# Batch 1's time-shift mix moved from TensorE to VectorE in a fused attention and channel-mix kernel

## The chip, the cores and the metric

The kernel runs on one core of a Trainium2 chip. The metric is the device time of one execution in microseconds; the kernel before was timed three times, and the median stands for it. Engine names as in the profile: PE (TensorE matmul), PEld (its weight loads), DVE (VectorE), ACT (ScalarE), POOL (GpSimd), SP (SyncE, which here only issues DMAs).

## The reference

Eight batches, 8 heads, 576 positions, head size 64; d_model 512, d_ff 1024. Linear attention, and then a channel mix with a time shift:

```python
q_s = softmax(q over the head dimension); k_s = softmax(k over the positions)
kv  = einsum('bhsd,bhse->bhde', k_s, v)
x   = einsum('bhsd,bhde->bhse', q_s, kv)        # -> (B, S, 512)
x_prev = x shifted by one position, zeros first
xk = mu_k * x + (1.0 - mu_k) * x_prev
xr = mu_r * x + (1.0 - mu_r) * x_prev
k  = np.maximum(xk @ w_k, 0.0)
v  = k * k @ w_v
r  = 1.0 / (1.0 + np.exp(-(xr @ w_r)))
out = r * v
```

## The kernel before

**Groups and units.** Attention is worked off in 16 groups of four heads, named by batch and half: group 31 is batch 3, second half. The channel mix is worked off in ten units of 512 positions (two of 256) over rings of four batches, `xk` and `xr`. Unit 1 needs batches 0 and 1, unit 2 batches 1 and 2, and so on.

**Steps of a group** (b, g stand for batch and half, and a last 0 or 1 for a part):

- `load..q`, `load..k`, `load..v`: loads into the 11 buffers `raw`, two halves of 288 KB each for batches 0 and 1, one load of 576 KB for the others (issued by POOL from batch 1 on, L204).
- `expq`, `expk` (ACT, L328), `cast` of v (ACT, L334); `rsum`, `rrec`, `scale` (DVE): the softmax of q.
- `T`: 18 or 36 small transposes of q on PE (L367); `KV`: the products of k and v, which also give the sum of exp k (L397). In batch 0 they are separate; later both stand in one block, named `TKV` or `B`, in one PSUM buffer `att` (there are two).
- `rz`, `w` (DVE): kv divided by the sums; `qt` (ACT, L375): the transposed q out of PSUM. From batch 5 on q is transposed by a DMA that SP issues (L517), and `qt` is that DMA.
- `X` (PE, L537): x = w times qt, 8 matmuls. It rides in the block `B` of the next group, ahead of that group's transposes; for groups in `ALONE` it stands by itself (X21, X71).
- `xs`, `xb` (ACT, L546, L543): x out of PSUM; `edge`, `diff` (DVE, L551, L555): the shifted difference; four scalings by mu, `sc` (DVE, L560), and two adds, `mix` (DVE, L565), give `xk` and `xr`.

**Fused batches.** In batches 0 and 1 (`FUSED`) the mix is folded into the weights instead: DVE or POOL multiplies kv by mu and 1 - mu (`kvn`, `wp`, L475), PE computes xk and xr directly with 16 matmuls each (`X100`, `X101`, ..., L487), the shifted half reading qt one column earlier, and ACT and DVE copy the results out (`x1000`, `x1001`, ..., L497). Here `edge` is a copy within qt.

**Steps of a unit**: `k10` to `k17` (PE, L621, four matmuls of 128x512 each, in the first two units partly in two halves, the second named `k10.2`), `relu` (ACT, L608), `sq` (DVE, L612); `r10` to `r13` (PE, L653), `th` (ACT, L658); `v100`, `v101`, ... (PE, L673, four matmuls each; in unit 0 v is cut by `WV`), `o` (DVE, L679) and the stores `st` (SP, L689). The banks of PSUM for k, r and v are the four `mm`.

**Order.** Nothing is scheduled at run time: `ORDER` is a list of all steps written out. Each engine issues its own steps in the order of the list, and waits there for what a step needs. A number behind a step's name is the buffer that it takes. So a step that waits holds back everything behind it on its engine. `muload` fetches mu for the scalings, `mu` transposes it on PE, `mucopy` takes it out of PSUM.

The functions that the diff touches:

Of the kernel before, what the change touches and what calls it, by code (L numbers as in the profile page):

```python
# [8 lines left out]
ACT = mybir.ActivationFunctionType  # L9
# [21 lines left out]
WV = (0, 4, 6, 8)  # L31
# [5 lines left out]
FUSED = (0, 1)  # L37
EARLY_UNITS = 2
ALONE = ((2, 1), (B - 1, 1))
# [5 lines left out]
ACT!load00q0:0 zero ident load00q1 ACT!load00k0:1 load01q1:2 ACT!load01q0 rows load00v consts warm  # L45
load00k1 load01v late load01k0:3 load10q0:4 wk00 wk01 expq001:0 expq000 load11q0:5 rsum001:0
ACT!load01k1 rsum000 load10k0:6 expq011:1 rrec001 wk11 rrec000 rsum011:1 fill:1 fill.2:2 fill.3:3
fill.4:0 fill.5:1 fill.6:2 fill.7:3 fill.8:0 fill.9:1 fill.10:2 fill.11:3 fill.12:0 fill.13:1
fill.14:2 fill.15:3 fill.16:0 wide:0 scale000:0 expq010 expk000:0 rsum010 expk001 scale001
widecopy wk10 rrec010 fill.17:1 fill.18:2 KV001:0 rrec011 scale010:1 KV000 T00:1 rest Z00 qt00:0  # L50
scale011 rz00:0 expk010:1 fill.19:3 fill.20:1 fill.21:1 T01:3 edge00 kvn00:0 load10q1 expk011
fill.22:1 KV010:2 wp000:0 expq100:2 wr wp001 X000:1.0 qt01:1 KV011 x0001 Z01 load10k1 x0000 rz01:1
X001:0.3 kvn01:1 wp010:1 k02:0 x0010 edge01 k00:1 x0011 X010:1.0 load11q1 k03:2 x0100 x0101 k01:3
wv0 rsum100:2 k00.2 expk100:2 load10v1:7 k02.2 wp011 expq110:0 k03.2 relu00:0 k01.2 load10v0
X011:0.1 relu01:1 k07:1 sq01:0 load11v0:8 sq00 expq101 k05:3 load11v1 relu02:2 rsum101 relu03:1
k06:0 rrec100 sq02 relu05:0 sq03 x0110 k04:2 x0111 relu06:2 sq05 load11k1:9 r00:3 relu07:1
load11k0 expk101 r02:0 expq111 wv1 r03:1 relu04:0 rsum111:3 th00:0 r01:2 sq07 th03:1 sq04 rrec101
th02:2 scale101:2 v020:3 wv2 scale100 cast101:0 v030:1 load20v0:10 rrec111 cast100 scale111:0
muload v000:0 th01:3 rsum110 cast110:1 v010:2 load20q0:0 rrec110 cast111 scale110 TKV10:0
expk111:0 load21q0:2 expk110 load30q0:1 rz10:2 kvn10:0 TKV11:1 qt10:2 wp100:0 load20k0:3 v011  # L60
load21v0:4 rz11:0 sq06 v031 kvn11:1 edge10 qt11:0 v021 wp110:1 load61v0:6 v001 v032 edge11 v002
cast200:2 X100:0.1 load21k0:5 o00 v022 load31q0:7 x1001 x1000 v012 o02 expq200:1 wp111 mu:0
X110:1.0 mucopy k13:3 load30v0:8 x1101 x1100 k11:0 wp101 o01 expq210:2 k13.2 rsum200:0 k11.2
load31k0:9 relu13:1 X111:0.1 relu11:0 load40q0:10 k12:2 x1111 x1110 k17:3 o03 expk200:1 load30k0:0
sq11:1 k10:0 st03.2 sq13 k16:1 st00 expq300:0 rrec200 rsum210:1 load40v0:2 st03 X101:1.0 st01
relu17:2 k12.2 x1011 st00.2 x1010 k10.2 load31v0:3 sq17 relu16:0 k14:3 scale200:1 relu10:1
relu12:2 r12:1 cast210:0 sq10 load60q0:1 TKV20:0 rsum300:2 relu14:1 r11:0 th12:4 rrec210 rrec300
load41q0:4 rz20:1 expk210:2 k15:2 sq12 w20:0 scale210:2 r10:3 qt20:1 v120:1 sq16 relu15:2
scale300:0 expq310:1 B21:1.0 load50q0:5 sq14 th10:5 v110:2 rz21:2 sq15 xs20:0 xb20 w21:1
load40k0:7 rsum310:3 v100:3 qt21:0 v121 edge20 diff20:0 th11:6 v111 cast300:1 sc2000:0 X21:0.1  # L70
sc2011:1 o11 r13:0 xs21:1 load41k0:8 xb21 sc2010 o12 v101 expk300:0 edge21 rrec310 r20:2 diff21:1
expk310:1 load41v0:0 sc2001 v130:1 sc2101:2 mix200 th20:1 load60v0:9 TKV30:1 sc2100 th13:0
sc2111:0 mix210 v131 cast310:2 sc2110 k27:2 cast400:0 o13 load51q0:3 rz30:0 k21:0 scale310:1
st13.2 relu27:0 load50k0:2 st13 expq400:2 k22:1 o10 k20:2 w30:2 relu22:1 load71v0:10 st10 mix201
qt30:2 st11 k23:3 sq27:0 st11.2 rsum400:0 relu21:2 k24:1 st01.2 relu23:0 st10.2 B31:0.1 mix211
expk400:2 sq23 k26:0 rz31:1 relu24:0 rrec400 load50v0:7 sq21 xb30:0 w31:0 k25:3 sq24 scale400:2
relu20:2 r22:1 xs30 qt31:1 sq20 r23:2 edge30 diff30:0 relu25:0 B40:1.0 relu26:2 sq22 sc3001:2
expq410:0 v200:3 sc3000 mix300 th22:0 v220:0 load71k0:4 rz40:2 sq25 th23:6 rsum410:1 xs31:1 r21:1
xb31 v230:2 sq26 expq500:1 edge31 sc3011:1 v201 diff31:1 cast410:1 load61q0:5 w40:1 v231 sc3101:0
sc3100 th21:3 rrec410 load61k0:0 mix310 v221 expq510:2 o23 r30:1 o20 qt40:0 load71q0:3 k33:2  # L80
scale410:0 st20.2 th30:5 st20 k37:3 relu33:1 st12.2 o22 k40:1 st12 relu37:0 sc3111:2 v210:2 sc3010
st02 expk410:0 rsum500:2 st02.2 k41:0 k35:3 expq600:0 load51k0:8 mix301 v211 sc3110 relu40:2
load51v0:1 sq37:1 k32:1 relu35:0 o21 expk500:1 sq33 B41:0.1 mix311 relu41:1 load70q0:2 sq35 k31:3
rz41:0 sq40:0 relu32:0 w41:2 sq41 k30:2 sq32 relu31:2 rsum510:3 cast500:2 k34:0 r31:1 relu30:1
rsum600:0 load70v0:7 relu34:0 r33:3 th31:1 sq30 xs40:0 rrec510 k36:2 xb40 rrec500 sq31 sq34 k44:0
scale500:1 relu36:1 r32:1 relu44:2 k43:2 edge40 qt50:1 th32:4 diff40:0 v330:0 qt41:2 sq36 v310:1
rrec600 st23.2 sc4001:0 th33:2 scale510:2 v331 expq610:1 k46:3 sc4000 qt51:0 relu43:0 o33
load60k0:5 B50:1.0 relu46:1 cast510:0 scale600:0 k47:2 st23 k42:0 cast600:1 v300:3 load70k0:1 sq46
qt60:2 sq44 rz50:1 mix400 v311 relu47:1 xs41:1 xb41 v320:2 o31 relu42:2 sq47 v301 expq700:2 st31.2
edge41 sq42 diff41:1 st21 r41:1 st21.2 expk510:2 o30 v321 sc4101:1 st30.2 sc4100 sq43 st31 k45:0  # L90
sc4110:2 mix410 st30 r40:3 relu45:1 expk600:0 o32 v410:0 sq45 rsum610:1 th41:6 k50:2 sc4111 k52:1
relu50:2 w50:0 rsum700:2 cast610:2 v411 k51:2 relu52:0 o41 mix411 k53:1 relu51:1 rrec610 B51:0.1
sq51:1 sq50 k54:0 scale610:1 xb50:1 v400:2 relu53:1 sc4010:0 relu54:2 rz51:2 sq52 k55:1 expq710:0
sc4011 rrec700 mix401 v401 relu55:0 rsum710:3 k56:0 th40:3 expk610:1 k57:1 sq53 sq54 relu56:1 sq55
r50:3 w51:1 relu57:2 scale700:2 r51:0 th50:1 cast700:0 v500:1 rrec710 o40 sq56 v510:3 th51:5 st40
sq57 xs50 st41 edge50 B60:1.0 st33 diff50:1 v501 st32.2 xb51:0 sc5000:1 st41.2 rz60:0 sc5001 v511
xs51 st40.2 w60:2 expk700:2 mix500 qt61:1 r52:2 o50 expk710:0 o51 B61:0.1 st50 edge51 v520:0
st50.2 sc5010:2 diff51:0 th52:6 st22 r53:1 cast710:1 st51 sc5011 sc5100:0 st51.2 sc5101 v521
sc5110:1 th53:3 mix510 v530:3 sc5111 rz61:1 mix511 k60:2 o52 xb60:0 v531 w61:0 st52 mix501
relu60:0 st32 k61:1 scale710:0 xs60 st52.2 B70:1.0 st22.2 relu61:1 o53 k62:0 xb61:1 sq60:0 st53  # L100
edge60 k63:2 relu62:2 st53.2 diff60:1 xs61 st33.2 k64:1 sq61 relu63:0 qt70:0 sc6000:0 sc6001 k65:3
sc6010:1 relu64:1 mix600 k66:0 sq62 edge61 relu65:2 sq63 k67:2 diff61:0 relu66:0 r60:1 sq64
sc6100:2 relu67:1 sc6101 r61:3 sq65 th60:1 mix610 v600:0 sq66 th61:5 sc6011 sq67 v610:2 sc6110:0
sc6111 mix601 v601 mix611 v611 rz70:2 w70:1 r62:1 o60 o61 st60 r63:3 th62:4 st60.2 v620:0 st61
th63:6 v630:2 v621 v631 o62 k70:1 st62 o63 k71:3 relu70:2 st63 st63.2 k72:0 sq70:1 relu71:0 qt71:2
k73:2 sq71 relu72:1 k74:1 sq72 relu73:2 k75:3 sq73 relu74:0 k76:0 sq74 relu75:1 k77:2 sq75
relu76:2 r70:1 sq76 relu77:0 B71:0.1 sq77 th70:0 v700:3 xb70:0 rz71:0 w71:2 r71:0 v701 th71:3 xs70
v710:2 o70 edge70 X71:1.0 st70 diff70:1 v711 xb71:1 st70.2 sc7000:2 r72:1 sc7001 xs71 o71 r73:0
edge71 st71 th72:2 mix700 st71.2 v720:3 diff71:0 th73:1 sc7010:1 v730:2 sc7100:0 sc7101 sc7110:2
v721 mix710 sc7111 v731 sc7011 o72 k80:1 mix711 st72 k81:0 st72.2 o73 relu80:1 mix701 st73 k82:3  # L110
relu81:2 st73.2 sq80:0 k83:2 sq81 relu82:0 k84:1 sq82 relu83:1 k85:0 sq83 relu84:2 k86:3 sq84
relu85:0 k87:2 sq85 relu86:1 r80:1 sq86 relu87:2 r81:0 sq87 th80:5 v800:3 th81:4 v810:2 v801 v811
o80 r82:1 st80 o81 st80.2 r83:0 th82:6 st81 st81.2 v820:3 th83:0 v830:2 v821 v831 o82 k90:1 st82
o83 k91:0 st82.2 relu90:0 k92:3 st83 relu91:1 sq90:1 k93:2 relu92:2 sq91 st83.2 k94:1 relu93:0
sq92 k95:0 relu94:1 sq93 k96:3 relu95:2 sq94 k97:2 relu96:0 sq95 r90:1 relu97:1 sq96 sq97 r91:0
th90:3 v900:3 th91:2 v901 v910:2 o90 v911 st90.2 st90 v910.2:1 o91 v911.2 st91.2 st91 o91.2 st91.3
st91.4
"""


class Slot:

# [728 lines left out]
```

## Time and profile before

| | |
|---|---|
| three runs | 195.72, 196.65, 196.67 us; median 196.65 |
| profiled execution: span from first to last instruction | 194.9 us, 1.75 less than the median (its own time is not given besides the span) |
| granted PE clock | 1.00 throughout |
| PE, DVE, ACT, POOL busy | 184.8, 150.1, 141.0, 43.6 us |
| HBM | 33.56 MB read, 9.44 MB written |
| k of unit 0 begins (k02), X21, X71, last matmul | 15.6, 55.95, 158.6, 191.2 us |

The rows of the profile read: line, engine, operation, output<-inputs, shape, count, then busy time and mean, then the idle time of the engine before them and what ended it. A line of the timeline begins with start and duration. In the table by stage each engine has its busy microseconds and the number of instructions in brackets; then come the granted clock, the mean share of the 16 DMA engines, and GB/s. In the list of DMA issues the last number is the median time from issue to landing.

### The profile page before, as it was taken

The numbers are of one execution on the slowest core, as the hardware profiler recorded it, in microseconds if no ns is written. First come the engines' busy times: TensorE is split into PE (matmuls) and PEld (weight loads), VectorE is DVE, ScalarE is ACT, GpSimd is POOL, SyncE is SP. The second block draws the span as 40 slices with busy tenths as digits, with TensorE's granted clock in tenths as the row PEclk, the third lists the DMA queues.
The fourth block names the chain that finished last, engine by engine and source line by source line (L and its number), as shares of the span: only waits on it lengthen the run. The fifth ranks groups of instructions, "written<-read, shape, count | busy, mean of one in ns | idle before, by whom it ended". The sixth has DMA issues, their size and how long they took to land.

```text
span 194.9 us, 4739 instructions
## 1 busy us (share of the span) xinstructions
PE 184.8 (95%) x1849; PEld 90.6 (46%) x1873; DVE 150.1 (77%) x347; ACT 141.0 (72%) x218; POOL 43.6 (22%) x70
## 2 busy tenths in 40 slices
PE   7789999999999999999999999999999989999992
PEld 2264445435544554545554444444444434444751
DVE  1887668799999999989989998999924359622532
ACT  3788899899999999989996798677226632662340
POOL 8444457794324212241110000000000000000000
PEclk9999999999999999999999999999999999999999
DMA  6999999999999999999699604886039872403413
GB/s 185 322 263 294 268 346 302 402 393 394 411 389 392 392 408 335 290 366 316 143 217 124 203 0 108 170 190 146 0 73 116 56 89 54 111 0 79 95 43 108
DMA packets 23586, 41.86 MB, mean 215 GB/s; under 512 B 9344, under 2 KB 12684, under 8 KB 23564
## 3 DMA queue, kind: packets, MB, share of 16 engines
q0 software_dynamic: 9440, 27.99, 45.3%
q1 hardware_dynamic: 13308, 12.13, 28.4%
q10 hardware_dynamic: 816, 1.44, 2.0%
q8 instruction: 14, 0.23, 0.6%
q14 instruction: 8, 0.07, 0.1%
HBM read 33.56 MB, written 9.44 MB: 221 GB/s over the span
## 4 chain that ended last, share of the span: by engine, by line
PE 76%; DMA 15%; POOL 2%; issue 2%; ACT 1%; DVE 1%; POOLq 0%; DVEq 0%
PE mm_c L673 10%; PE mm_d L673 9%; PE mm_c L621 8%; PE mm_b L621 7%; PE mm_a L621 7%; PE mm_b L653 7%; PE mm_d L621 6%; DMA wk_ab<-in_moe_w_k_dram 6%; DMA wv_a<-in_moe_w_v_dram 5%; PE mm_a L673 5%; PE mm_b L673 4%; DMA raw_k<-in_v_dram 4%; PE mm_a L653 4%; PE mm_d L653 3%; PE mm_c L653 1%
## 5 line engine op out<-in xcount | busy, mean ns | idle before, releaser
L673 PEld LDWEIGHTS <-k_a 128*128 128x128 bf16 x144 | 13.8, 98 | 16.6 <-issue 0.5
L653 PEld LDWEIGHTS <-xr 128*128 128x128 bf16 x144 | 13.9, 98 | 16.1 <-issue 0.2
L673 PEld LDWEIGHTS <-k_b 128*128 128x128 bf16 x152 | 14.4, 98 | 15.0 <-issue 0.2
L653 PE MATMUL mm_b<-wr,xr 128*128 128x512 bf16 x62 | 16.3, 379 | 0.1
L621 PEld LDWEIGHTS <-wk_ab 128*128 128x128 bf16 x80 | 7.7, 98 | 8.3 <-issue 0.8
L621 PEld LDWEIGHTS <-wk_bb 128*128 128x128 bf16 x80 | 7.8, 98 | 7.7
L621 PEld LDWEIGHTS <-wk_aa 128*128 128x128 bf16 x80 | 7.4, 98 | 8.2 <-issue 0.9
L621 PEld LDWEIGHTS <-wk_ba 128*128 128x128 bf16 x80 | 7.5, 98 | 7.8 <-issue 0.2
L653 PE MATMUL mm_a<-wr,xr 128*128 128x512 bf16 x35 | 9.2, 380 | 0.1
L673 PE MATMUL mm_c<-wv_a,k_a 128*128 128x512 bf16 x32 | 8.2, 379 | 0.0
L608 ACT ACTIVATE rel_a<-mm_b 128x512 bf16<-128x512 f32 (+1 forms) x8 | 4.6, 579 | 4.2 <-PE mm_b L621 3.6
L608 ACT ACTIVATE rel_b<-mm_b 128x512 bf16<-128x512 f32 (+1 forms) x7 | 4.1, 585 | 4.9 <-PE mm_b L621 4.8
L621 PE MATMUL mm_c<-xk,wk_aa 128*128 128x512 bf16 (+1 forms) x26 | 7.3, 363 | 0.0
L612 DVE TENSOR_TENSOR k_a<-rel_b 128x512 bf16<-128x512 bf16 (+1 forms) x14 | 5.3, 382 | 2.5 <-ACT rel_b L608 2.5
L673 PE MATMUL mm_d<-wv_a,k_b 128*128 128x512 bf16 x26 | 7.1, 379 | 0.1
L653 PE MATMUL mm_d<-wr,xr 128*128 128x512 bf16 x28 | 7.2, 379 | 0.0
L621 PE MATMUL mm_c<-xk,wk_ab 128*128 128x512 bf16 (+1 forms) x24 | 6.9, 362 | 0.0
L612 DVE TENSOR_TENSOR k_b<-rel_a 128x512 bf16<-128x512 bf16 (+1 forms) x14 | 5.5, 392 | 1.8 <-ACT rel_a L608 1.3
L608 ACT ACTIVATE rel_c<-mm_a 128x512 bf16<-128x512 f32 (+1 forms) x11 | 6.2, 561 | 0.7 <-PE mm_a L621 0.7
L612 DVE TENSOR_TENSOR k_b<-rel_b 128x512 bf16<-128x512 bf16 (+1 forms) x14 | 5.5, 392 | 1.3 <-ACT rel_b L608 0.9
L612 DVE TENSOR_TENSOR k_b<-rel_c 128x512 bf16<-128x512 bf16 (+1 forms) x12 | 4.7, 392 | 1.9 <-ACT rel_c L608 1.6
L621 PE MATMUL mm_d<-xk,wk_bb 128*128 128x512 bf16 (+1 forms) x22 | 6.1, 360 | 0.1
(352 smaller groups left out, 532.3 us busy)
## 6 DMA issues: line engine op xcount, KB each, us to landing
out_dram<-th_b SPq DMA_DIRECT2D x12, 128.0 KB, 3.6
out_dram<-th_g SPq DMA_DIRECT2D x12, 128.0 KB, 5.2
out_dram<-th_d SPq DMA_DIRECT2D x11, 128.0 KB, 5.6
out_dram<-th_a SPq DMA_DIRECT2D x10, 128.0 KB, 2.7
raw_k<-in_v_dram POOLq DMA_DIRECT2D x2, 576.0 KB, 8.9
raw_c<-in_q_dram POOLq DMA_DIRECT2D x2, 576.0 KB, 7.0
raw_b<-in_q_dram POOLq DMA_DIRECT2D x2, 576.0 KB, 10.4
raw_f<-in_k_dram POOLq DMA_DIRECT2D x2, 576.0 KB, 7.9
```

The source lines that it names most:

```text
L608: kn.nc.scalar.activation(out=kn.rels[rel.index][:, 0:n], in_=kn.bank(kf)[:, 0:n], func=ACT.Relu, scale=HALF_ROOT)
L612: kn.nc.vector.tensor_tensor(out=kn.k2s[k2.index][:, fc, 0:n], in0=kn.rels[rel.index][:, 0:n], in1=kn.rels[rel.index][:, 0:n], op=ALU.mult)
L621: kn.nc.tensor.matmul(kn.bank(kf)[:, 0:n], lhsT=kn.wk[fc // 4][ct % 2][:, ct // 2, (fc % 4) * 128: (fc % 4) * 128 + 128], rhs=kn.xs[0][:, ...
L653: kn.nc.tensor.matmul(kn.bank(rps), lhsT=kn.xs[1][:, ct, c:c + 128], rhs=kn.wr[:, ct, :], start=(ct == 0), stop=(ct == CT - 1))
L673: kn.nc.tensor.matmul(kn.bank(vps)[:, 0:width], lhsT=kn.k2s[k2.index][:, ft, 128 * m:128 * m + 128], rhs=wv_of(ft)[:, part], start=(ft == ...
```

## The change

1. `FUSED` holds groups 00 and 01 only. Batch 1's groups take the steps of the later batches: `w`, `X` with 8 matmuls, `xs`, `xb`, `edge`, `diff`, four `sc`, two `mix`. X10 rides in the block B11; X11 stands alone.
2. The transposes of both groups of batch 1 go into one block (`SOON`): TKV10 holds the transposes of group 10, those of group 11 (into the other `att` buffer) and KV10. B11 holds X10 and KV11. The copy qt11 depends on TKV10 alone.
3. w_v is loaded in four pieces of two row blocks each, not three, and v of unit 0 is computed in four pieces per tile.
4. The loads of mu for the scalings go from POOL's queue to SP's, and they and `mu` stand earlier.
5. The whole `ORDER` is another one: loads, attention steps, unit steps and stores stand in other places, and other buffers are taken.
6. `HALF`, a mixed form, is empty and has no effect.

```diff
-WV = (0, 4, 6, 8)
+WV = (0, 2, 4, 6, 8)
-FUSED = (0, 1)
+FUSED = ((0, 0), (0, 1))
+HALF = ()
+SOON = {(1, 1): (1, 0)}
-ALONE = ((2, 1), (B - 1, 1))
+ALONE = ((1, 1), (2, 1), (B - 1, 1))
...
-            kn.nc.gpsimd.dma_start(out=kn.mu_sb[4 * m:4 * m + 4, :], in_=bass.AP(
+            kn.nc.sync.dma_start(out=kn.mu_sb[4 * m:4 * m + 4, :], in_=bass.AP(
...
-    mu_load = add("POOL", emit_mu_load, name="muload")
+    mu_load = add("SP", emit_mu_load, name="muload")
...
+        own = Slot("any" if b == 0 else "att")
+        turns[b, g] = [transpose_q, before_t, own, qs, None]
+        yield
+        soon = [turns[t] for t in SOON if SOON[t] == (b, g)]
+        done = turns[b, g][4]
...
-            qtp = kvp = Slot("att")
+            qtp = kvp = own
+            first_t = not crossed and not done
...
-                if not crossed:
+                if first_t:
                     transpose_q(qtp)
+                for t in soon:
+                    t[0](t[2])
                 kv(qtp)
...
-            qcopy = add("ACT", lambda: copy_qt(qtp), [tr, wdone], [qt], [qtp], name=f"qt{tag}")
+            qcopy = add("ACT", lambda: copy_qt(qtp), [done] if done else [tr, wdone], [qt], [qtp], name=f"qt{tag}")
```

The new order, around the steps that the prediction follows (batch 1's attention; then the loads of group 31 and X21):

```
... r00:2 r03:3 scale100 th00:0 scale111 cast100:0 sq05 mucopy th03:1 cast101 sq07 expk100 r01:0 r02:2
TKV10:1.0 v020:3 th01:2 expk110:0 sq06 cast111:1 cast110 rz10:2 w10:0 qt10:2 v000:1 load20k0:0 v030:0
load20q0:2 expk111 qt11:0 B11:1 rz11:0 v001 v021 w11:1 xs10:0 xb10 edge10 diff10:0 sc1001:0 load30q0:1
v031 sc1000 th02:3 load21k0:3 load41q0:4 load21q0:5 X11:0.1 xs11:1 v002 v003 o00 load21v0:7 xb11 v010:2
cast200:2 edge11 diff11:1 v011 v032 load30v0:6 v022 mix100 sc1101:1 load61q0:8 v033 v012 k12:1 expk200:1
v013 v023 expq200:1 load31q0:9 sc1100 o03 mix110 o02 o01 k13:0 k12.2 k13.2 ...
... th20:6 rsum300:3 sq14 expq310:1 B21:0.1 rz21:2 sq15 xb20:0 xs20 st03 r10:1 w21:0 v121 load40q0:9
qt21:2 rsum310:2 edge20 rrec300 v110:3 th12:2 X21:1.0 th10:3 v100:0 v101 ...
```

In the new order B71, r61, v600, v521, v620, v601, v621, r63, k75 and X71 follow each other on PE; in the old one B71, v700, r71, v701, v710 and X71. The eight stores of unit 0 (st03.2, st01.2, st01, st02, st00.2, st02.2, st00, st03) are the first stores on SP; in the old order five of them came first (st03.2, st00, st03, st01, st00.2), and the others behind stores of unit 1.

## The prediction

> **What bounds the kernel now.** I read the page first: its busy shares, then the 40 slices.
>
> ```profile
> span 194.9 us, 4739 instructions
> PE 184.8 (95%) x1849; PEld 90.6 (46%) x1873; DVE 150.1 (77%) x347; ACT 141.0 (72%) x218; POOL 43.6 (22%) x70
> ...
> PE   7789999999999999999999999999999989999992
> DVE  1887668799999999989989998999924359622532
> ...
> DMA  6999999999999999999699604886039872403413
> ```
>
> PE is full from about 15 us to 191 us, DVE from 40 to 140, the DMA engines from 5 to 90. So a PE microsecond saved counts only if DVE and the loads keep up. The table by stage gives DVE's reserve:
>
> ```profile
> 42.60:61.00 18.40, 18.08 (x276) 8.86 (x279) 17.94 (x39) 18.40 (x27) 7.33 (x11) 1.00 1.04 398
> 61.00:97.00 36.00, 35.79 (x439) 18.11 (x441) 35.03 (x73) 34.54 (x52) 9.18 (x14) 1.00 0.93 328
> ```
>
> From 42.6 to 97 us DVE idles 0.46 + 0.97 = 1.43 us, PE 0.53, and DMA (share about 1) moves 390 to 410 GB/s. Only one PE wait after 40 us is large; it stands in the timelines of PE and of SP's queue:
>
> ```profile
> 158.65 0.22 PE L537 MATMUL att_a<-qt_c,w_c 64*64 64x64 bf16 x4 [0.85 <-DVE xd_b L555]
> ```
>
> ```profile
> 147.87 5.32 SPq L517 DMA_TRANSPOSE qt_c<-qs_a  x1
> ```
>
> This is X71. The DVE write that it needs (w71) ended long before; what ended late is qt71, the transposing DMA, whose issue took 5.32 us where the other five took 1.3 to 1.5. Last, the timeline of ACT and the DMA issues from 36 to 56 us, since the new order moves loads there:
>
> ```profile
> 51.44 1.23 ACT L328 ACTIVATE eq_b<-raw_h 128x1152 bf16<-128x1152 f32 x1
> ...
> 53.11 1.11 ACT L543 CAST xb_a<-att_a 128x1024 bf16<-128x1024 f32 x1
> 54.02 1.23 ACT L375 COPY qt_a<-att_b 128x1152 bf16<-128x1152 bf16 x1
> ```
>
> ```profile
> raw_h<-in_q_dram POOLq DMA_DIRECT2D x1, 576.0 KB, 10.5
> raw_i<-in_v_dram POOLq DMA_DIRECT2D x1, 576.0 KB, 11.1
> raw_j<-in_k_dram POOLq DMA_DIRECT2D x1, 576.0 KB, 11.4
> ```
>
> raw_h is q of group 31: issued at 38.08, landed 10.5 us later at 48.56, used at 51.44 (expq310). raw_j, issued at 41.23, landed at 52.6. ACT runs in order: xb20 and qt21 queue behind expq310, and X21 on PE needs qt21.
>
> **Part by part.**
>
> PE, batch 1's X. X111 starts at 40.48 behind two matmuls that began at 39.95; k12 starts at 41.09. 41.09 - 39.95 - 0.43 = 0.71 us for each of four, 2.84 us. Instead X10 rides in B11: B21 takes 0.96 (51.43 to 52.39), TKV20 0.78, so 0.2; X11 alone costs what X21 does, 0.4. PE saves 2.84 - 0.6 = 2.2 us. Moving T11 into TKV10's block shifts 0.37 us and saves one switch of about 0.1.
>
> DVE. Per group go two evictions (L497, 0.757 each), one pair of weight products (L475, 0.50), the 0.45 edge of qt; there come an edge of xb (0.19), diff (0.756), four scalings (0.362 each), two mix adds (0.75 each). 3.89 - 2.46 = 1.43, for two groups 2.9; neighbours overlap by 0.09 and six instructions are added, so 2.9 less up to 0.5: 2.7 us in a stretch with little reserve. ACT trades two 0.64 copies for xs and xb (0.3 + 1.05): nothing. POOL loses two product pairs (1.75 us), mere room there. The mu transpose on PE (0.15) moves ahead of r00; its two 2 KB loads go to SP, which then waits for nothing but its own first loads and has no store until 39 us: zero, one extra queue entry if that cover fails (0.6 each).
>
> Start, to k12.2. Up to 20.8 us both kernels do the same on PE, with wk01 and the x copies at the same places: 0 (half a microsecond either way, since expq110 now waits for its load at 17.07 ahead of x0100). Then four k, mu and four r follow (eight times 0.86 and 0.15: 28.0), and TKV10 now comes ahead of v. It needs both halves of exp k and of the v casts; ACT has expk101, th00, cast100, th03, cast101, expk100 to do from 25.0, 3.4 us at 0.6 and 0.5 us each, so 28.4: PE waits 0.4. v020 needs wv0, which now stands behind seven more half loads: wr landed at 23.54, the first half load 1.06 behind, the others 0.75 apart, 29.1, and a quarter of wv takes 1.2: 30.3, and PE waits 0.8. B11 needs expk111, behind th01, expk110, two casts and a 1.0 us qt copy: 32.3, PE waits 0.7. X11 needs xb10, 34.4. Then X11 (0.4) and twelve half pieces (0.43 each) cover DVE's edge10 to mix110: 0.11 + 0.67 + 0.56 + 0.6 + 0.11 + 0.67 + 0.67 + 0.56 + 0.6 + 0.67 = 5.2 us from 34.45, 39.7; PE reaches k12.2 at 40.0, no wait. From there to X21 are 14.7 us of PE work and three switches: 55.0, if nothing holds it. In the kernel before X21 starts at 55.95, and behind it stand the same matmuls in both. So 0.95 us would be won here: 2.2 less 1.9 of new waits, plus what the old order lost in the switches and waits that go.
>
> The load that spoils it. In the new order load31q0 is the tenth load after load20v0 instead of the eighth; the same bytes stand ahead of load20v0, so 36.08 holds for it. One load takes 1.50 us (seven landings, each issue plus its time to landing, from 37.76 to 46.74). Unit 0's stores also come sooner: o00, o03, o02, o01 end by 41 us, so all eight go out between 39 and 45 us, where before it was five between 42.66 and 46. Those five cost the loads landing from 46.7 to 52.6 together 1.4 us. Ten loads and eight such stores: 36.08 + 15.0 + 8 x 0.28 = 53.3. Between the bounds of 51.1 (stores free) and 53.8 (1.05 MB at 390 GB/s, 2.7 us) I take 53.4, because the tenth place itself landed at 52.6 with five stores. The Trainium skill, DMA: Bandwidth & Descriptors, section Where 436 GB/s comes from, puts HBM traffic of one core at some 358 GB/s, by which, as an estimate, 0.37 us a store would make it 54.0; the trace moved 390 to 410, and the measurement decides.
>
> ACT reaches expq310 at 51.6 (qt20 and th20 end then). Behind it stand expq310 1.06, xb20 0.92, xs20 0.16, qt21 1.02 and a hand-over of 0.1: X21 at 53.4 + 3.3 = 56.7, against 55.0 wanted. PE has nothing else to run there. So X21 is 0.8 us later than before, not 0.95 earlier.
>
> X71. The new order issues qt71 and B71 among units 6 and 7, with r61, v600, v521, v620, v601, v621, r63 and k75 (7 us) ahead of X71 instead of four pieces. The 0.9 us go; if the transposing DMA is slow again, up to 0.9 stays.
>
> DVE later on. When mix110 ends (39.7) DVE still owes o02, o01, three scalings, two mix adds, 3.4 us, so 43.1; the kernel before reached the same sum at 42.63 + 0.67 (x1011) - 1.26 (rsum200, already done) = 42.0. It is 1.1 behind, then idles about 1.0 for the sums of expq310, while PE itself is 0.8 late: 1.4 too late net, if its idle time stays. I let 1.0 vanish in the 1.43 of idle and book 0.4; the ends are 0 and 1.4.
>
> wv in quarters and its extra semaphores: the same bytes; booked in v020's wait.
>
> **Sum.** +0.8 (X21) - 0.9 (X71) + 0.4 (DVE) = +0.3 us. It is made against the profiled execution, whose span is 194.9; the median of the three runs is 196.65, 1.75 above, and I carry that over: 196.65 + 0.3 = 196.9. A measurement of this kernel tells about 0.5% (1.0 us) from no change.
>
> **Rivals.**
>
> Gain holds. Load31q0 lands by 51.6, because stores give way or the loads start sooner. For it: only 1.8 us separate 53.4 from harmless, and before every late use had 2 us in hand. Against: the DMA share is 1 throughout. Then X21 at 55.0: -0.95 - 0.9 + 0.4, 195.2.
>
> DVE becomes the bound (slower). The extra 2.7 us fall into the stretch from 40 to 97 us, where mix210, mix211 and mix310 gate k26, r21 and k47. For it: 1.43 us of idle is all the reserve, and much of it is waiting for a relu. Against: idle time shrinks when an engine is late. It decides once less than 1.0 of the idle vanishes; in full it costs 1.4: 196.65 + 0.8 - 0.9 + 1.4 = 197.9. The Trainium skill, VectorE: DVE Perf Modes, section Rules for kernel authors, tells authors to minimize the number of chained DVE operations, which speaks against this change; by it the time would be this rival's. The trace agrees as far as it goes: 3.9 us a group in ten operations against 2.5 in five.
>
> Transposes stall again. X71's wait, or one like it at B60 to B71, stays, because any of the six transposing DMAs can be as slow as qt71: 196.65 + 0.8 + 0.4 = 197.8.
>
> **How the numbers follow.** Forecast 0.38 (own range 195.7 to 197.6, by the bounds 51.1 and 53.8 and half a microsecond at the start), gain holds 0.28, DVE 0.24, transposes 0.10. Faster by over 0.5%: 0.28 + 0.02 of the forecast's edge = 0.30. Slower: 0.20 of DVE, 0.06 of transposes, 0.04 of the forecast = 0.30. Within: 0.40. The range leaves a fifth outside: 195.0 to 198.6.
>
> **What would show it.** Right: eq_b<-raw_j with ACT idle some 1.8 us before it, released by that load, near 53.4; X21 near 56.7; no X71 wait; DVE some 2.7 us busier. Wrong: expq310 starting straight behind th20 (gain holds); PE waits released by xk or xr of L586 (DVE); PE waits at B5 to B7 with a long DMA_TRANSPOSE row (transposes); PE waits of over 2.5 us in sum between 27 and 40 us (my walk of the start).

## The result and the profile after

The changed kernel takes 201.48 us (median of four runs, 201.26 to 202.04), against 196.19 us for the kernel before (median of four runs, three of them those given above): 1.0263 times as long, 95% interval 1.0231 to 1.0295. The forecast was 196.9 us, its range 195.0 to 198.6; the time lies above the range. The profiled execution after took 202.04 us with a span of 200.3, so as much lies around the span as before (1.74 against 1.75). Runs of one kernel differ by up to 2 us with PE's clock, whole or halved for 3.4 us at a busy place, which is why some medians below are split by the granted clock.

The page of the changed kernel, for the rows shown of before, and the row of the granted clock:

```profile
span 200.3 us, 4635 instructions
...
PE 188.1 (94%) x1825; PEld 91.1 (46%) x1825; DVE 152.2 (76%) x353; ACT 138.9 (69%) x218; POOL 41.4 (21%) x65
...
PE   7899986899999999999995999999999999999991
...
PEclk9969999999999999999998799999999999999999
```

PE has two holes that the kernel before did not have: a 6 in the seventh slice (30 to 35 us) and a 5 in the 22nd (105 to 110 us). Beside and behind the second one the granted clock falls; before it was 1.00 throughout. (The 6 at 10 us is a halved clock too, while PE has little to do.) The table by stage shows the second hole:

```profile
42.60:61.00 18.40, 17.99 (x215) 8.43 (x213) 17.80 (x35) 17.84 (x26) 5.41 (x8) 1.00 1.04 401
61.00:97.00 36.00, 36.00 (x498) 18.89 (x497) 35.71 (x82) 35.03 (x53) 10.51 (x15) 1.00 0.93 328
97.00:140.00 43.00, 40.54 (x343) 18.53 (x342) 37.36 (x82) 31.26 (x47) 1.45 (x2) 0.96 0.46 106
```

From 42.6 to 97 us PE idles no more than before (0.41 us against 0.53); from 97 to 140 PE idles 2.46 us and its clock is 0.96 (42.37 of 43 us busy at 1.00 before). The timeline of PE names every large wait (start, duration, then in brackets the idle time ahead and what ended it); the last line is the matmul that was X71's wait before:

```profile
30.13 0.59 PE L696 MATMUL mm_d<-wv_a,k_a 128*128 128x512 bf16 x2 [0.81 <-DMA wv_a<-in_moe_w_v_dram]
33.38 0.22 PE L558 MATMUL att_a<-qt_c,w_a 64*64 64x64 bf16 x4 [1.79 <-ACT qt_a L379]
36.05 0.22 PE L558 MATMUL att_b<-qt_a,w_b 64*64 64x64 bf16 x4 [0.55 <-ACT xb_a L564]
...
108.00 0.22 PE L558 MATMUL att_b<-qt_c,w_c 64*64 64x64 bf16 x4 [2.46 <-DMA qt_c<-qs_a]
...
110.28 1.91 PE L676 MATMUL mm_d<-wr,xr 128*128 128x512 bf16 x4
...
149.86 0.22 PE L558 MATMUL att_b<-qt_a,w_b 64*64 64x64 bf16 x4
```

In order: v020 waits for wv0, B11 for the copy qt11, X11 for xb10, and B51 waits 2.46 us for a transposing DMA. Behind that the four matmuls of r41 take 1.91 us. X71, the last line, no longer waits. SP's queue shows why B51 waits:

```profile
97.40 1.42 SPq L538 DMA_TRANSPOSE qt_b<-qs_b  x1
...
101.70 1.82 SPq L538 DMA_TRANSPOSE qt_c<-qs_a  x1
```

The first is qt51, the second qt50. In the kernel before qt50 is the first of the three that are issued there, and B51 has no wait (timelines of SP's queue and of PE):

```profile
93.00 1.39 SPq L517 DMA_TRANSPOSE qt_b<-qs_b  x1
...
109.76 0.22 PE L537 MATMUL att_a<-qt_b,w_a 64*64 64x64 bf16 x4
```

B51 carries X50, which needs qt50; qt51 is needed one block later, in B60. The new order makes the half that is needed second first: scale510 stands ahead of scale500, and qt51 ahead of qt50. So qt50 is issued at 101.70 and lands at 107.95, where PE is ready for it at 105.5. In the kernel before, 16.8 us lie between its issue and B51.

**Where the 5.4 us of span lie.** X21 starts at 57.30, 1.35 later than before:

```profile
57.30 0.22 PE L558 MATMUL att_a<-qt_c,w_a 64*64 64x64 bf16 x4 [0.35 <-ACT qt_c L379]
```

The last piece of v (v910.2) starts at 195.19, 5.02 later. From the time when PE is ready for B51 to the start of B60 the changed kernel needs 8.45 us, and 4.25 in the run without the wait (below): 4.2 us, of which 2.46 are the wait and 1.74 the slow matmuls behind it. X71's wait is gone (0.85). 1.35 + 4.2 - 0.85 is 4.7; another 0.3 lies spread behind X21, and the end, from v910.2 on, is 0.4 longer (5.1 against 4.7). A step starts here with its first matmul. The recorded expectations mostly give the start of its first weight load, 0.1 us ahead of that, and 0.4 to 0.6 ahead where the step waits (56.7 for an X21 at 57.09, 35.2 for an X11 at 35.82).

### The profile page after: what moved, and what is told of

It reads as the page before. It is cut to its first block, busy times and chain, and to the rows that moved or that the text cites. A ratio compares the mean times of both kernels' runs of the same rounds, so it can differ in the third digit from the quotient of the medians.

```text
span 200.3 us, 4635 instructions
## 1 busy us (share of the span) xinstructions
PE 188.1 (94%) x1825; PEld 91.1 (46%) x1825; DVE 152.2 (76%) x353; ACT 138.9 (69%) x218; POOL 41.4 (21%) x65
## 4 chain that ended last, share of the span: by engine, by line
PE 61%; ACT 13%; DVE 11%; DMA 9%; issue 3%; SPq 1%; ACTq 0%; DVEq 0%
PE mm_c L644 7%; PE mm_a L644 6%; PE mm_b L644 6%; PE mm_a L696 6%; PE mm_d L696 6%; PE mm_b L696 5%; PE mm_d L644 5%; PE mm_c L696 4%; DMA raw_b<-in_k_dram 3%; DMA qt_c<-qs_a 3%; PE mm_d L676 3%; PE mm_c L676 3%; DMA out_dram<-th_a 3%; PE mm_a L676 3%; PE mm_b L676 2%
## 5 line engine op out<-in xcount | busy, mean ns | idle before, releaser
L676 PE MATMUL mm_c<-wr,xr 128*128 128x512 bf16 x40 | 10.3, 379 | 0.0
L631 ACT ACTIVATE rel_a<-mm_c 128x512 bf16<-128x512 f32 (+1 forms) x10 | 5.7, 574 | 5.6 <-PE mm_c L644 5.5
L635 DVE TENSOR_TENSOR k_a<-rel_c 128x512 bf16<-128x512 bf16 (+1 forms) x15 | 5.9, 390 | 2.0 <-ACT rel_c L631 1.6
L644 PE MATMUL mm_c<-xk,wk_ba 128*128 128x512 bf16 (+1 forms) x26 | 7.3, 363 | 0.0
L644 PE MATMUL mm_c<-xk,wk_bb 128*128 128x512 bf16 (+1 forms) x26 | 7.3, 362 | 0.0
L635 DVE TENSOR_TENSOR k_a<-rel_a 128x512 bf16<-128x512 bf16 (+1 forms) x16 | 6.2, 390 | 0.4
L581 DVE TENSOR_SCALAR xm_b<-xd_b,mu 128x576 bf16<-128x576 bf16 x18 | 6.4, 384 | 0.1
L644 PE MATMUL mm_a<-xk,wk_ab 128*128 128x512 bf16 (+1 forms) x20 | 6.2, 394 | 0.0
L676 PE MATMUL mm_b<-wr,xr 128*128 128x512 bf16 x24 | 6.2, 379 | 0.0
L644 PE MATMUL mm_a<-xk,wk_aa 128*128 128x512 bf16 (+1 forms) x20 | 6.1, 389 | 0.0
```

The costliest lines, as they stand in the source:

```text
L581: kn.nc.vector.tensor_scalar(out=kn.xms[xms[m].index][:, u, :], in0=kn.xds[xd.index][:, u, :], scalar1=kn.mu[:, c:c + 1], scalar2=None, op ...
L631: kn.nc.scalar.activation(out=kn.rels[rel.index][:, 0:n], in_=kn.bank(kf)[:, 0:n], func=ACT.Relu, scale=HALF_ROOT)
L635: kn.nc.vector.tensor_tensor(out=kn.k2s[k2.index][:, fc, 0:n], in0=kn.rels[rel.index][:, 0:n], in1=kn.rels[rel.index][:, 0:n], op=ALU.mult)
L644: kn.nc.tensor.matmul(kn.bank(kf)[:, 0:n], lhsT=kn.wk[fc // 4][ct % 2][:, ct // 2, (fc % 4) * 128: (fc % 4) * 128 + 128], rhs=kn.xs[0][:, ...
L676: kn.nc.tensor.matmul(kn.bank(rps), lhsT=kn.xs[1][:, ct, c:c + 128], rhs=kn.wr[:, ct, :], start=(ct == 0), stop=(ct == CT - 1))
```

## The experiments

The theory: the late qt50 and the halved clock behind it cost some 4 us, and without them the kernel is about where the forecast had it. The rivals: VectorE's extra load is the cause and B51 only the place where it shows; the transposing DMA is slow there whatever is done; the half clock costs nothing by itself. Kernels that ran side by side share their runs of the kernel before. Its median was 195.97, 196.63, 196.06 and 195.84 us in the four sets, so kernels of different sets are compared by their ratios.

### The halves of batch 5 exchanged

```diff
-... rsum500:2 relu30:0 rrec510 rrec500 ... rz50:1 scale510:1 ... th31:5 scale500:0 ... qt51:1 ... th40:4 qt50:2 ... B51:1.0
+... rsum500:2 relu30:0 rrec500 rrec510 ... rz50:1 scale500:0 ... th31:5 scale510:1 ... qt50:2 ... th40:4 qt51:1 ... B51:1.0
```

> The changed kernel (201.5) with the two halves of batch 5 in the order in which TensorE needs them: scale500 and its transposing DMA qt50 trade places in the order with scale510 and qt51. Theory (late transpose): B51 held TensorE for 2.46 us because qt50 is issued at 101.70, and the granted clock was halved for 3.4 us right behind that wait; with qt50 issued at about 97.4 both are gone: no wait at B51, clock 1.0 after the start, 197.3 (4.0 to 4.5 less). Rival (VectorE's extra 2 us are the cause, and B51 only the place where TensorE's lead shows): the wait moves to qt51 at B60 or to another step, and the time stays at 200 or more. Rival (the transposing DMA is slow by itself at this place): qt50 lands 6 us or more after its issue and the wait is cut by less than half, 199.5 to 200.5.

Measured: 197.69 us, 1.0085 times the kernel before (1.0055 to 1.0114), 3.8 less than the changed kernel's median and, by the two ratios, 3.5 less. Its timeline of PE has no wait at B51 nor at B60 (the second line), and its clock is 1.00 until the last matmul:

```profile
105.28 0.22 PE L555 MATMUL att_b<-qt_c,w_c 64*64 64x64 bf16 x4
...
109.53 0.22 PE L555 MATMUL att_a<-qt_b,w_a 64*64 64x64 bf16 x4
```

qt51 now is the late one (issued at 101.40, landed at 107.19) and harms nobody, since B60 begins at 109.53. The order of two halves was 3.5 to 3.8 of the 5.3 us. Neither rival holds: the wait went nowhere else, and qt50, issued at 97.21, had landed by 105.28.

### Filling the wait with work

```diff
-FILLS = 22
+FILLS = 34
-... mix410 sq44 B51:1.0
+... mix410 sq44 fill.23:0 fill.24:0 ... fill.34:0 B51:1.0
```

> The changed kernel with 12 matmuls of 128x512 whose result nobody reads put on TensorE directly ahead of B51, some 2.6 us of work that the computation does not need, in the place where TensorE waits. It prices the halved clock apart from the wait. Theory (the wait costs 2.5 us, and the halved clock behind it 1.5 more): the filled time is waiting time anyway, the clock stays 1.0 after the start, and the kernel takes 1.3 to 1.7 less, 199.8 to 200.2. Rival (the clock is halved for another reason, or its halving costs nothing as other engines bind there): 201.5, or more by what the fill exceeds the wait (0.2).

Measured: 200.21 us, ratio 1.0205 (1.0169 to 1.0241), 1.3 less than the changed kernel's median (1.1 by the ratios). Timeline of PE:

```profile
105.77 2.75 PE L296 MATMUL mm_a<-still 128*128 128x512 bf16 x12
108.45 0.22 PE L557 MATMUL att_b<-qt_c,w_c 64*64 64x64 bf16 x4
...
110.01 1.03 PE L675 MATMUL mm_d<-wr,xr 128*128 128x512 bf16 x4
```

B51 begins 0.45 us later than in the changed kernel, and yet the kernel is faster than that median, because r41's four matmuls take 1.03 in place of 1.91. So there idling cost more than useless work: the halved clock has a price of its own, 1.1 to 1.3 and the 0.45, near the 1.74 of the trace.

### The two loads later in the list

```diff
-... r40:3 load71v0:6 relu44:1 ... relu53:2 load70v0:7 ...
+... B51:1.0 load71v0:6 load70v0:7 st33 ...
```

> The changed kernel with load71v0 and load70v0 (576 KB each, issued 2.9 and 1.3 us ahead of qt50) moved behind B51 in the order. Theory that these loads stretch the transposing DMA from its 3.3 us alone to the 6.25 seen: qt50 lands by 105.3, B51 waits for less than 0.3, no half clock, 197.3 to 197.8. Theory that it takes 6 us by itself at this place, or waits for qt51 ahead of it on its queue: no change, 201.3 to 201.7. The loads are needed 10 us later, so holding them costs nothing.

This one missed its aim. GpSimd issued the loads at 98.64 and 100.18, as early as in the changed kernel (98.84 and 100.38): a place in the list binds only steps of one engine, and GpSimd waits for free buffers, not for B51. So it is the changed kernel again, and as such it told something. In its profiled execution B51 waited 2.01 us for qt50, and the clock was not halved: 199.72 us, 1.8 less than the changed kernel's median, of which 0.45 is the shorter wait. A second run at a clock of 0.999 took 199.65; the two at 0.983 took 201.77 and 200.10 (median of the four 199.91, ratio 1.0216, 1.0161 to 1.0271). The lower clock is thus worth 0.4 to 2.1 us here. It also bounds the two results above: against its runs at the whole clock, exchanging the halves is worth 2.0 us, the length of the wait, and filling the wait gains nothing.

### The same loads issued by SP behind qt50

```diff
-load71v0:6 ... qt50:2 ... load70v0:7
+qt50:2 SP!load71v0:6 SP!load70v0:7
```

> The changed kernel (201.5) with load71v0 and load70v0 issued by SP behind qt50, not by GpSimd ahead of it (the run that moved them in the list alone left them at 98.64 and 100.18, since GpSimd does not wait for TensorE). Theory (the loads stretch the transposing DMA, which takes 3.3 us alone): qt50 lands by 105.3, B51 waits for less than 0.3, the clock stays whole, 197.4 to 198.0. Rival (it takes 5.8 us at this place whatever else runs): B51 waits for 2.0 to 2.5 as before, 199.7 without and 201.5 with the halved clock.

Measured: 197.57 us, ratio 1.0063 (1.0034 to 1.0093). SP's queue:

```profile
101.77 1.30 SPq L536 DMA_TRANSPOSE qt_c<-qs_a  x1
103.24 0.46 SPq L205 DMA_DIRECT2D raw_g<-in_v_dram  x1
103.87 0.39 SPq L205 DMA_DIRECT2D raw_h<-in_v_dram  x1
```

qt50 is issued at the same time as in the changed kernel, but B51 starts at 105.54 without a wait: the DMA needed at most 3.8 us with both loads issued behind it, and 6.25 and 5.8 in the two profiles where the two loads of 576 KB had been issued 2.9 and 1.3 us ahead of it. qt51 stood ahead of it on SP's queue in all three. So lateness and loads issued ahead were both needed for the wait; taking away either one ends it.

### Group 11's transposes back in B11

```diff
-SOON = {(1, 1): (1, 0)}
+SOON = {}
-TKV10:1.0 ... expk111 qt11:0 B11:1 rz11:0 v001 v021 w11:1 xs10:0
+TKV10:1 ... expk111 B11:0.1 rz11:0 v001 v021 w11:1 qt11:0 xs10:0
```

> The changed kernel with the transposes of group 11 back in B11 (TKV10 holds T10 and KV10 alone; qt11 behind w11), so that B11 does not write into the buffer from which qt11 is still being copied. Theory: B11's wait of 1.79 us falls to some 0.7 (expk111 ends at 32.3), T11's 0.37 us move from TKV10 to B11, X11 has to wait for qt11 as well, and X11 begins at 35.0 to 35.7 in place of 36.05; with B51's wait unchanged the kernel takes 0.3 to 1.0 less, 200.5 to 201.2. Rival (X11 is set by qt11 either way, as ACT has the same copies in another order): no change within 0.3.

Measured: 201.07 us, ratio 1.0245 (1.020 to 1.029); its one run without a half clock took 199.92, where the changed order without it took 199.65 and 199.72. These runs show no gain, as the rival said. Timeline of PE:

```profile
31.56 0.22 PE L555 MATMUL att_a<-qt_c,w_a 64*64 64x64 bf16 x4 [0.30 <-ACT qt_c L376]
...
35.68 0.22 PE L555 MATMUL att_b<-qt_a,w_b 64*64 64x64 bf16 x4 [1.50 <-ACT xb_a L561]
```

B11's wait fell from 1.79 to 0.30, but X11 now waits 1.50. It begins 0.37 us earlier than in the changed kernel, and only 0.14 earlier than with the halves exchanged (35.82), where the start is the changed kernel's. ACT now makes qt11 ahead of xb10, and idles 1.33 us for w11 before it.

### Group 11's copies on VectorE, and an earlier load of q of group 31

Both stand on the kernel with the halves exchanged. The casts of group 11's v are changed like its qt copy.

```diff
-                kn.nc.scalar.copy(out=to[:, :, 64:64 + S],
+                (kn.nc.vector.tensor_copy if (b, g) == (1, 1) else kn.nc.scalar.copy)(out=to[:, :, 64:64 + S],
-qcopy = add("ACT", lambda: copy_qt(qtp), [done] if done else [tr, wdone], ...)
+qcopy = add("DVE" if done else "ACT", lambda: copy_qt(qtp), [done] if done else [tr, wdone], ...)
...
```

> The kernel with the halves of batch 5 exchanged (197.7, X21 at 56.7), and on top of it the two casts of group 11's v and the copy qt11 on VectorE in place of ScalarE. Theory (the start is bound by ScalarE's queue, which is full from 24.9 to 33.1, so that qt11 ends at 33.10 and B11 waits 1.9 for it): B11's wait falls below 0.5, X11 begins at 33.3 to 33.8 in place of 35.2. Then load31q0, which landed at 52.4, is late after all: X21 at 55.7 to 56.0, 196.7 to 197.0. If the load holds nothing: X21 at 55.0, 196.0. Rival (VectorE gives the time back, as 2.4 us are put on it): X21 at 56.5 or later, 197.5 to 197.9.

Measured: 199.77 us, ratio 1.0164 (1.0108 to 1.0221). The time says nothing of the edit: in all four runs the granted clock was 0.976 to 0.989, in the profiled one halved from 10.1 to 16.9 us, so that k02 began at 19.00 (15.98 without). What the profile shows is that B11 no longer waits for qt11.

```diff
-... load30v0:6 v022 mix100 sc1101:1 load61q0:8 ... expq200:1 load31q0:9
+... load31q0:9 load30v0:6 v022 mix100 sc1101:1 load61q0:8 ... expq200:1
```

> The same as the run with group 11's copies on VectorE, and load31q0 two places earlier among the loads (ahead of load30v0 and load61q0), which brings its landing from 52.4 to some 49.5. Theory (with the start mended, the load sets X21, as the prediction's step had it): X21 at 55.0, 0.7 to 1.0 less than without this edit, 195.8 to 196.1. Rival (the load has no part): X21 and the time as without it, within 0.3.

Measured: 197.45 us, ratio 1.0051 (1.0029 to 1.0073). X11 starts at 34.09 in place of 35.82, X21 at 55.12 in place of 57.09: the start had lost 1.7 us at X11 and 2.0 at X21 to ACT's queue. Whether the early load was needed for that stays open, as the run to compare with was disturbed; ACT was free for expq310 at 51.33, and the load in its old place landed at 52.4 to 52.9. But v910.2 starts only 0.97 earlier. Of the other 1.0 us, 0.58 went to the next late load; timelines of PE and of ACT:

```profile
64.31 0.59 PE L641 MATMUL mm_c<-xk,wk_aa 128*128 128x512 bf16 x2 [0.58 <-ACT rel_a L628]
```

```profile
62.61 1.15 ACT L335 CAST vv_a<-raw_f 128x1152 bf16<-128x1152 f32 x1 [1.28 <-DMA raw_f<-in_v_dram]
```

raw_f is v of group 31. ACT waits for it, and the relus queue behind.

### Less work for VectorE behind X21

```diff
-            xdiff = add("DVE", diff, [o], [xd], name=f"diff{tag}")
+            less = (b, g) == (2, 0)
+            xdiff = o if less else add("DVE", diff, [o], [xd], name=f"diff{tag}")
...
-name=f"sc{tag}{m}{u}") for u in range(2)]
+name=f"sc{tag}{m}{u}") for u in range(0 if less else 2)]
```

> The kernel with the halves of batch 5 exchanged (197.7), with the difference and the four scalings of group 20 left out (its mix adds x to the shifted x): 1.8 us of VectorE's work just behind X21, about what the change put on this engine. Theory (VectorE's load is what the stretch behind X21 lost, 0.84 us in the profile where the prediction booked 0.4): the time falls by 0.5 to 1.0, to 196.7 to 197.2. Rival (VectorE has room there, and the loss lies in the start alone): 197.5 to 197.8.

Measured: 197.59 us, ratio 1.0055 (1.0029 to 1.0081). The kernel that it stands on has 1.0085 (1.0055 to 1.0114) from another set, and the kernel of its own set that has all of VectorE's work and no wait at B51, the one with the loads behind qt50, took 197.57: the times do not show a gain, nor do they exclude 0.6 us. In its profiled execution the stretch from X21 to r32 came out 0.3 us shorter, but then k42 waited 1.07 us for a th that was held by a store (ACT idled 1.18 for it). So by the profile this share of VectorE's load accounts for 0.3 us, where the prediction had booked 0.4 for all of it.

### w_v in three pieces, and x0100 ahead of expq110

Both stand on the kernel with the halves exchanged, one edit each. In the first, wv3, v003, v013, v023 and v033 leave the order as well.

```diff
-WV = (0, 2, 4, 6, 8)
+WV = (0, 4, 6, 8)
```

> The kernel with the halves of batch 5 exchanged (197.7), and w_v again in three pieces (the first of four row blocks, as in the kernel before). Theory (the quarters' work is done in waiting time): v020 waits 1.2 longer for its larger piece, to 31.0, and v000 and v030 take 0.43 more each, but B11 waits for qt11 until 33.1 in any case, so its 1.9 shrink by as much: 197.5 to 198.0. Rival (the quarter is what keeps the start together): k12.2 later by 0.8 or more, 198.4 or more.

Measured: 198.80 us, ratio 1.0112 (1.0049 to 1.0174), in two groups: 197.85 and 197.89 at a clock of 1.0, 199.70 and 199.95 at 0.983. At the full clock the quarters are worth next to nothing, as the theory had it, since B11 waits in any case. Its profiled execution is of the other group. The table by stage shows the 3.41 us behind v020's wait:

```profile
31.54:34.95 3.41, 3.41 (x9) 1.22 (x8) 0.00 (x0) 1.73 (x3) 2.17 (x3) 0.50 1.14 334
```

The larger piece holds v020 for 2.23 us, and the clock is 0.50 in the window that follows. In the profile, then, the quarters' worth is that they divide a wait: with them v020 waits 0.72 and B11 1.88, and the clock stays whole.

```diff
-... x0101 wp011 expq110:2 k02:1 k00:2 rsum110:2 x0100 wv0 ...
+... x0101 wp011 x0100 expq110:2 k02:1 k00:2 rsum110:2 wv0 ...
```

> The kernel with the halves of batch 5 exchanged (197.7), and x0100 put ahead of expq110 on ScalarE again, as in the kernel before. Theory (expq110 waits for its load until 17.02 and holds x0100, so that k00.2 loses 1.0 where the kernel before lost 0.4): k00.2 goes 0.4 to 0.6 earlier, but B11 still waits for qt11, whose chain on ScalarE begins with expq110's half, so that little of it is left at X21: 197.2 to 197.7. If all of it is kept: 197.1.

Measured: 197.93 us, ratio 1.0073 (1.0038 to 1.0108). The four runs at a clock of 0.996 or more took 196.90 to 197.18, so all of the 0.5 us is kept there; the six others took 197.78 to 198.75. In the profiled one, one of the six, B11's wait had grown from 1.88 to 2.04 us, and the clock was halved behind it. A gain of half a microsecond made another wait longer, and in most runs that took it back: the ratio, 1.0073, is not told apart from 1.0085.

### All of it together, and the end

On the run with the copies on VectorE and the early load of q: load31v0 ahead of load50q0, x0100 ahead of expq110.

> The run with group 11's copies on VectorE and the earlier load31q0 (197.45 and 0.2 to 0.9 above the kernel before; in its profile X21 at 54.75, but ScalarE then waited 1.28 us for load31v0 ahead of cast310, which held k21 by 0.74), with two more places changed: load31v0 ahead of load50q0, and x0100 ahead of expq110 on ScalarE. Theory (what is left is waits of the order, not VectorE): the wait ahead of cast310 falls below 0.3 and k21 goes unheld, the wait of k00.2 at 18.5 falls by 0.4, the last matmul piece starts at 188.6 to 189.0 in place of 189.72, and the kernel takes 196.2 to 196.6, level with the kernel before or 0.3 below it on the same chip. Rival (VectorE is full from 30 to 97 us and takes the place of each wait removed): 197.2 to 197.6 as without the two edits.

Measured: 196.39 us, ratio 1.0010 (0.9983 to 1.0037): level with the kernel before. No wait ahead of cast310, none at k21. v910.2 starts at 189.03, 1.14 us earlier than in the kernel before, but the end from there on is 5.7 us long, not 4.7. In its DMA queues between 191 and 194 us stands an instruction fetch, beside the last stores:

```profile
q10 hardware_dynamic: 221, 0.22, 23.0%
q1 hardware_dynamic: 163, 0.13, 13.5%
q14 instruction: 1, 0.01, 1.5%
```

```diff
     def emit_warm():
+        for _ in range(3):
+            kn.nc.scalar.activation(out=kn.warm[:], in_=kn.warm[:], func=ACT.Exp)
```

> The combined run (196.39, level with the kernel before; last matmul piece at 188.93 against 190.06 before, but 5.8 us from there to the end against 4.8), with three more 1x1 activations on ScalarE at its start, where it waits for its first load. In the profiles with group 11's three copies taken from ScalarE an instruction fetch (queue q14) lies at 191.7 to 193.2, among the last stores; in those with the copies on ScalarE it lies 1 to 2 us ahead of them. Theory (ScalarE's instruction stream is three shorter, so its last block is fetched while it issues the last stores, and they wait for it): the fetch moves ahead of the stores, the end is 5.2 us behind the last piece, and the kernel takes 195.6 to 195.9, 0.2 to 0.5 less than the kernel before on the same chip. Rival (the fetch has no part in it, the stores themselves are slower): 196.2 to 196.5 as without the three.

Measured: 195.83 us, ratio 0.9981 (0.9964 to 0.9997). The fetch lies at 188.4, ahead of the stores, and the end is 5.1 us long again. So in the profile three instructions that do nothing took 0.6 us off the end; the two ratios differ by as much, but their intervals overlap. The other profiles agree: in the ten of the new order in which the fetch lies ahead of the last matmul, the span ends 4.0 us behind that matmul, and 4.7 to 4.9 in the three in which it lies behind it. With this the change is level with the kernel before; its lead of 0.2% is less than the 0.5% that a single measurement can tell.

## Why the prediction was wrong

**The step that failed** is the part on the new order and its transposing DMAs. The prediction followed one of them, qt71, found its wait gone, and booked nothing for the five others; it let a rival carry them, between B60 and B71, at 0.9 us and a chance of 0.10, as a matter of one DMA being slow by chance. It never set the place of each transposing DMA in SP's queue against the block that needs it. That would have shown qt51 ahead of qt50 with B51 needing qt50; in the result 3.8 us lie between qt50's issue and the time when PE is ready for it, where the kernel before had 16.8, and two loads go out just ahead. Measured: 2.46 us of wait and 1.74 of halved clock in the profile; 3.5 to 3.8 us by exchanging the halves. The second half of that price was on no list of the prediction at all: the granted clock was 1.00 throughout the profile before, and a wait's price was taken as its length.

**The walk of the start** was right in kind and 1.65 us short by the time of X11. Forecast and measured: TKV10 28.4 and 28.2 (without the 0.4 that it was to wait); v020 held 0.8 until 30.3, and 0.81 until 30.1; B11 at 32.3 behind expk111, but 33.4; X11 at 34.4, but 36.05; k12.2 at 40.0 without a wait, but 41.83, held 0.2 by mix110, which ended at 41.78 and not at 39.7. The term that was missed is a buffer, not an input. B11's X10 and KV11 write the `att` buffer in which T11's transposes lie until qt11 has copied them out, and qt11 comes behind expk111 on ACT:

```profile
31.61 0.71 ACT L332 ACTIVATE ek_a<-raw_j 128x576 bf16<-128x576 f32 x1
32.19 1.13 ACT L379 COPY qt_a<-att_a 128x1152 bf16<-128x1152 bf16 x1
```

The prediction listed B11's inputs only. "Over 2.5 us of waits between 27 and 40" was the sign that it gave for a wrong walk; they came to 3.15, and the largest, B11's, is the hole in the seventh slice of the page.

**X21 came out near the forecast for a wrong reason:** 57.30 against 56.7. The chosen cause, load31q0 landing at 53.4 with ACT idle for 1.8 us ahead of expq310, did not occur. The load landed at 52.71, inside the bounds that were given (51.1 to 53.8), and ACT came to it later than that, straight behind th20, without idling, at 53.53 where the prediction had it ready at 51.6:

```profile
53.05 0.60 ACT L681 ACTIVATE th_g<-mm_d 128x512 f32<-128x512 f32 x1
53.53 1.17 ACT L332 ACTIVATE eq_b<-raw_j 128x1152 bf16<-128x1152 f32 x1
...
56.13 1.12 ACT L379 COPY qt_c<-att_a 128x1152 bf16<-128x1152 bf16 x1 [0.36 <-DVE w_a L418]
```

X21 was late because k12.2 began 1.8 us later than booked, and because X21 itself was held 0.4 us by qt21, which waited for w21: 55.0 + 1.8 + 0.4 = 57.2. Two errors of opposite sign met, and that the number came out near is luck.

**X71** was right: its wait went, and no other took its place there.

**VectorE** was booked at 0.4 with ends 0 and 1.4. It grew by 2.1 us (forecast 2.7). In the run with the halves exchanged, X21 to v910.2 takes 133.71 us against 134.22 before, less the 0.85 of X71: 0.34 us are lost behind X21. Leaving out 1.8 us of VectorE's work gave back 0.3 there in the profile. So the 0.4 was about right. (The prediction's ten operations a group are eight: edge, diff, four scalings and two adds; their sum of 3.89 us holds.)

So without the late qt50 the time lies in the stated range: 197.69 with the halves exchanged and 197.57 with the loads behind qt50. It is still 0.9 to 1.4 us above the sum, as the ratios are 1.0085 and 1.0063 where +0.3 us would be 1.0015. In the profile with the halves exchanged the span is 1.0 us longer than before: 1.14 at X21 (0.8 booked), -0.85 at X71, 0.34 behind X21, and 0.4 at the end, which was not booked and whose cause stays open.

## What to carry to other kernels

When an order is new, list for each DMA on the path its issue, the step that needs it and the distance between them, for all of them and not only for the one that was late before; where two halves of one batch are made in turn, the one needed first goes first. For each step list the buffers that it overwrites beside its inputs, with the copy that frees each. And a wait of TensorE is not priced by its length alone: in these runs one of 2 to 2.5 us could cost nearly twice its length, while two shorter ones in place of it (0.72 and 1.88) did not.

## What was not expected of the hardware

**The half clock has an edge, and a grid.** The clock's records in these traces change only at multiples of 3.413 us. In the ten windows behind 13 us in which PE idled between 1.24 and 1.90 us, the next window ran at the full clock; in the four in which it idled 2.04, 2.18, 2.23 and 2.46 us, the next was at 0.50. The wait of 2.01 us that a boundary cut (1.52 in one window, 0.49 in the next) is among the ten. So a wait of 2 us can cost 1.7 us more or nothing, by where it falls in the grid, which fits the two groups of runs above. Ahead of 13 us this edge does not hold: there windows with 0.58 to 1.61 us of idle time were followed by a half clock in nine of the profiles, and one with 1.39 was not. Idle time alone is then not the measure; what else counts stays open. The Trainium skill, TensorE: Matmul & The Clock Gate, Part 1, says that the window is 3413 ns long and runs free of the kernel, and that the clock is halved after at least one idle window; the length agrees with these traces, but here a window idle for six tenths was enough.

**A transposing DMA of one group** took at most 3.8 us with two loads of 576 KB issued behind it, and 5.8 to 6.25 with them issued 2.9 and 1.3 us ahead of it.

**An instruction fetch among the last stores** went with an end 0.6 to 0.9 us longer, and where it falls changed with the number of ScalarE's instructions: with three more it lay ahead of the stores, and the end was 0.6 us shorter.
